# Other groupings of tokens in the loads, wider weight pieces and 128-row stores in a pooled attention with a feed-forward layer

## The chip, the cores and the metric

The kernel runs on one core of a Trainium2 chip. The metric is the device time of one execution in microseconds (us); the time before is the median of three runs.

## The reference

```python
def _attn_ref(q, k, v):                      # each [8, 8, 576, 64], float32
    B, H, S, D = q.shape
    pool = 8; Sp = S // pool                 # 72 pooled keys
    k_p = k.reshape(B, H, Sp, pool, D).mean(axis=3)
    v_p = v.reshape(B, H, Sp, pool, D).mean(axis=3)
    scores = np.matmul(q, k_p.transpose(0, 1, 3, 2)) / np.sqrt(D)
    attn = softmax(scores)                   # over the 72 pooled keys
    return np.matmul(attn, v_p)

def reference(q, k, v, moe_w_in, moe_w_out): # w_in [512, 2048], w_out [2048, 512]
    x = _attn_ref(q, k, v).transpose(0, 2, 1, 3).reshape(8 * 576, 512)
    h = x @ moe_w_in
    return (h * np.cos(h)) @ moe_w_out       # [4608, 512], float32
```

## The kernel before

The 4608 tokens are worked through in nine tiles of 512 (`TILE`), numbered t = 0 to 8. Tile t < 8 holds 512 of the 576 tokens of batch t; the remaining 64 tokens of each of the eight batches (`REST`) make up tile 8. A tile has an up stage (`up_mm`, L325: 64 matmuls of 512 columns with `w_in`, then cos on ScalarE at L332 and the product into `g_sb` on VectorE at L335) and a down stage (`down_mm`, L338: 64 matmuls with `w_out`, one block of 16 for each 128 tokens, called ms 0 to 3). `down_halves` (L344) splits a 128-row matmul of the down stage into two of 64 rows with results in different banks.

The attention of batch t + 1 is threaded into the down stage of tile t: the list `fill` says after how many down matmuls each piece is issued. For tiles 1 to 6 the order is `first_scores` after 4 matmuls, further `scores_of` at 11, 13 and 20, `values_rows` from 22 on. For tile 0 the list is longer, since batch 1's keys are pooled there too. Batch 0's attention is done ahead of everything, in the first 16 us. Each engine's queue runs in the order in which the program issues (`tc.manual_schedule`).

Loads: `load_q` brings a batch's q with 9 tokens (`ROW`) per partition and two heads side by side on the 128 partitions; `load_kv` brings keys or values with 8 tokens (one group to be pooled) per partition, 72 partitions, 8 heads after one another. They are issued on POOL's queue and cast to bfloat16 on the way. `w_in` comes in four pieces of 512 columns (`W_IN`), each in two requests. At most eight of POOL's requests are under way: the ninth waits for the first to land.

q is transposed by blocks of 128 columns, which hold two tokens of 64 elements each: `q_transpose_mm` (L214) on TensorE for batches 0 and 1, `q_transpose` (L206) by a transposing transfer on SP's queue for the others. After it, the lower 64 partitions of `qT` hold the even one of the two tokens and the upper 64 the odd one. `scores_mm` (L234) multiplies pooled keys `kk` (kept in both halves) with `qT`: for one head 256 columns from one half. With 9 tokens per partition a pair of heads begins at group 9 times the pair's number, an odd count of half-groups, so that half r alternates from pair to pair:

```python
pj, hp = divmod(h0 + i, 2)
g, r = divmod(ROW * pj + ORDER[c0 // 64], 2)
```

`scores_exp` (L244) takes exp on ScalarE, `values_rows` (L288 to L310) multiplies with the pooled values and sends the normalised rows to `xT` through a transposing transfer on SP's queue (L309). `k_transpose` (L185) makes `kk` from the pooled keys with another such transfer; for batch 1 `k_transpose_mm` (L192, copied at L194) does it on TensorE. POOL's `gate` (L493) waits for `kk` before it issues the next batch's loads. `down_out` (L347 to L358) copies a 128-token block out of PSUM into `o_sb` (six buffers) and stores it with two requests of 64 rows, each row of 2 KB; both are issued on SP's queue. In the last chunk (`last_chunk`, L366) the three pieces of a block go out on SP's and ScalarE's queues.

Of the kernel before, what the change touches and what calls it, by code (L numbers as in the profile page):

```python
# [19 lines left out]
def kernel(  # L20
# [22 lines left out]

    ORDER = (0, 2, 4, 6, 1, 3, 5, 7, 8)

# [14 lines left out]

    W_IN = ((0, 512), (512, 512), (1024, 512), (1536, 512))
    w_in_sb = [wpool.tile([128, KCH, n], BF16, name=f"w_in_sb{i}") for i, (c0, n) in enumerate(W_IN)]
# [26 lines left out]
    def kv_tile():  # L89
        return kvst.tile([128, 2 * H * POOL * D], BF16, name="kv_st", tag="kv_st")  # L90
# [9 lines left out]
    def q_tile(b):  # L100
        staged["q", b] = qst.tile([128, KCH, ROW, D], BF16, name="q_b", tag="q_b")

    def load_kv(b, which, src, h0=0, h1=H):

        if (which, b) not in staged:
            staged[which, b] = kv_tile()[:Sp].rearrange("p (i h t d) -> p i h t d", i=2, h=H, t=POOL)
        nc.gpsimd.dma_start(out=staged[which, b][:, 0, h0:h1].rearrange("p h t d -> p h (t d)"),
                            in_=src[b, h0:h1].rearrange("h (p t) d -> p h (t d)", t=POOL))

    def load_q(b):  # L110
        q_tile(b)
        load_even(staged["q", b], b, q)

# [13 lines left out]
    def w_in_cols(ki, fc):  # L127

        cg, r = divmod(fc, 4)
        return w_in_sb[cg][:, ki, :].rearrange("p (n r) -> p r n", r=4)[:, r]  # L130

# [56 lines left out]
    def k_transpose_mm(b, bank, h0, h1):  # L188

        ps = bank.bitcast(BF16)[:, 0:(h1 - h0) * Sp].rearrange("p (h n) -> p h n", n=Sp)  # L190
        for h in range(h0, h1):
            nc.tensor.matmul(ps[:, h - h0, :], kp2[b % 2][:Sp, h].rearrange("p s d -> p (s d)"), identity[:Sp, :Sp],  # L192
                             is_transpose=True)
        nc.vector.tensor_copy(out=kk[b % 2][:, h0:h1, 0:Sp], in_=ps)  # L194

    QB = KCH * ROW // 2

# [19 lines left out]
    def ex_col(u, i):  # L217

        (c0, n), (h0, nh) = u
        return (i // 2 % 2 * (nh // 2) + i // 4 * 2 + i % 2) * n  # L220

# [4 lines left out]
    def scores_mm(b, u, pair):  # L226
        (c0, n), (h0, nh) = u

        for i in [i + 2 * a for k in range(0, nh, 4) for i in (k, k + 1) for a in range(2)]:
            bank, c = divmod(ex_col(u, i), nh * n // 2)  # L230
            pj, hp = divmod(h0 + i, 2)
            g, r = divmod(ROW * pj + ORDER[c0 // 64], 2)
            ps = pair[bank][:Sp, c:c + n] if isinstance(pair, tuple) else pair[:Sp, bank, c:c + n]
            nc.tensor.matmul(ps.rearrange("p (g n) -> p g n", n=64),  # L234
                             lhsT=kk[b % 2][half[r], h0 + i, 0:Sp],
                             rhs=att["qT", b][half[r], g:g + n // 64, hp * 64:hp * 64 + 64])

    def scores_exp(b, u, pair):
# [3 lines left out]
        for src, c, m in ([(pair[:Sp, :, 0:w], 0, 2)] if not isinstance(pair, tuple) else  # L242
                          [(bank[:Sp, 0:w].unsqueeze(1), a * w, 1) for a, bank in enumerate(pair)]):
            nc.scalar.activation(out=ex[:, c:c + m * w].rearrange("p (a n) -> p a n", a=m), in_=src,  # L244
                                 func=ACTF.Exp, scale=scale / POOL)
        att["ex", b, u] = ex
# [40 lines left out]

    def values_rows(b, us_, blk, pair, m=128):  # L288

# [4 lines left out]
        for u in us_:  # L294
            (c0, n), (h0, nh) = u
            ex = att["ex", b, u]
            for i in range(nh):
# [10 lines left out]
        c = token(b, n0)  # L308
        nc.sync.dma_start_transpose(out=xT.rearrange("p e q n -> p (e q) n")[:, :, c:c + m],  # L309
                                    in_=x[:m].rearrange("p e h d -> p (e h d)"))  # L310

# [35 lines left out]
    def down_out(t, ms, ps, c0=0, queues=(nc.sync, nc.sync), other=None):  # L347
# [4 lines left out]
        else:  # L352
            nc.vector.tensor_copy(out=o[:, 0:n], in_=other)  # L353
            nc.vector.tensor_tensor(out=o[:, 0:n], in0=ps, in1=o[:, 0:n], op=ADD)
        rows_of = out.rearrange("(b p t) m -> b t p m", b=B, t=ROW)
        for i, rows in enumerate(half):
            b_, pos = (t, 2 * ms + i) if t < B else (2 * ms + i, ROW - 1)
            queues[i].dma_start(out=rows_of[b_, ORDER[pos], :, c0:c0 + n], in_=o[rows, 0:n])  # L358

# [28 lines left out]
    for rows in half:  # L388
# [4 lines left out]
                   allow_small_or_imprecise_dtypes=True)  # L393
    load_even(staged["q", 0], 0, q, 0, 2)
    load_even(staged["k", 0], 0, k, 2, 4)
    load_even(staged["q", 0], 0, q, 2, 4)
    load_even(staged["v", 0], 0, v, 0, 2)
# [18 lines left out]
    q_tile(1)  # L416
    for i in range(4):
        load_w_in(i)
    load_kv(1, "k", k, 0, 4)
    load_even(staged["q", 1], 1, q, 0, 2)  # L420
    load_w_out(0)
    load_kv(1, "k", k, 4, 8)
    load_w_out(1)
    load_even(staged["q", 1], 1, q, 2, 4)
    for i in range(2):
# [71 lines left out]
    for t in range(NT):  # L497
# [69 lines left out]
        if t == 0:  # L567
            fill = [(4, lambda: values_rows(0, [REST], 0, bk[0], 64)),
                    (12, lambda: k_transpose_mm(1, bk[1][:, 0, :], 0, 4)), (13, pool_k),
                    (16, scores_of((1, us[0], 0), (1, us[1], 1))), (22, late_q),  # L570
                    (26, lambda: k_transpose_mm(1, bk[1][:, 0, :], 4, 8)), (27, batch_2),
                    (29, scores_of((1, us[2], 0), (1, us[3], 1))), (29, pool_v), (49, sums_values),
                    (53, lambda: q_transpose(2)), (57, values_rest)]
        elif b < B:
# [90 lines left out]
```

## Time and profile before

| | |
|---|---|
| time, median of 3 runs (lowest to highest) | 292.0 us (291.92 to 293.37) |
| the profiled execution: time, span | 291.55 us, 289.4 us |
| TensorE clock granted | 0.999 |
| busy: PE, DVE, ACT, POOL | 281.9, 169.9, 142.2, 139.7 us |
| L325 (up), 576 matmuls | 126.1 us |
| L338 (down, whole array), 462 matmuls | 110.5 us |
| L234 (scores), 192 matmuls | about 15 us by their own ends |
| software queue (POOL's loads) | 18.07 MB, 40.1% of 16 engines |
| hardware queue (stores, transposes, first keys) | 18.10 MB, 34.5% |

Matmuls overlap, so the busy times of single ones add up to more than they take one after another; the chain of waits gives the time that each group took on the path. A queue's share is the time of its packets over 16 engines' span.

### The profile page before, as it was taken

The numbers are of one execution on the slowest core, as the hardware profiler recorded it, in microseconds if no ns is written. First come the engines' busy times: TensorE is split into PE (matmuls) and PEld (weight loads), VectorE is DVE, ScalarE is ACT, GpSimd is POOL, SyncE is SP. The second block draws the span as 40 slices with busy tenths as digits, with TensorE's granted clock in tenths as the row PEclk, the third lists the DMA queues.
The fourth block names the chain that finished last, engine by engine and source line by source line (L and its number), as shares of the span: only waits on it lengthen the run. The fifth ranks groups of instructions, "written<-read, shape, count | busy, mean of one in ns | idle before, by whom it ended". The sixth has DMA issues, their size and how long they took to land.

```text
span 289.4 us, 4907 instructions
## 1 busy us (share of the span) xinstructions
PE 281.9 (97%) x1989; PEld 147.1 (51%) x1989; DVE 169.9 (59%) x227; ACT 142.2 (49%) x142; POOL 139.7 (48%) x107
## 2 busy tenths in 40 slices
PE   7899999999999999999999999999999999999994
PEld 2655445555554555555555545554555454445444
DVE  5467849774757574658375737583666557216622
ACT  3786634678056904691369316841676066016400
POOL 8549525997973498369633993399000000000000
PEclk9999999999999999999999999999999999999999
DMA  7999999999976998696869976985603510230033
GB/s 151 196 202 208 207 194 166 202 136 179 193 148 86 179 142 181 90 162 128 166 70 167 160 150 103 175 146 116 131 1 74 119 36 2 50 82 14 0 72 74
DMA packets 58614, 36.60 MB, mean 126 GB/s; under 512 B 37984, under 2 KB 53344, under 8 KB 58592
## 3 DMA queue, kind: packets, MB, share of 16 engines
q0 software_dynamic: 18832, 18.07, 40.1%
q1 hardware_dynamic: 39520, 18.10, 34.5%
q8 instruction: 15, 0.25, 0.3%
q10 hardware_dynamic: 240, 0.13, 0.2%
q14 instruction: 7, 0.06, 0.1%
HBM read 36.70 MB, written 9.44 MB: 159 GB/s over the span
## 4 chain that ended last, share of the span: by engine, by line
PE 90%; DMA 6%; ACT 2%; DVE 0%; issue 0%; POOL 0%; POOLq 0%
PE bank L325 43%; PE obank L338 25%; PE bank L338 6%; PE obank L344 5%; DMA w_out_sb<-in_moe_w_out_dram 4%; PE bank L303 3%; PE bank L234 3%; DMA q_b<-in_q_dram 2%; PE bank L344 2%; ACT ex L244 1%; PE bank L366 1%; PE bank L272 1%; PE bank L263 0%; ACT cos L332 0%; DVE g_sb L335 0%
## 5 line engine op out<-in xcount | busy, mean ns | idle before, releaser
L332 ACT ACTIVATE cos<-bank,half_pi 128x1024 f32<-128x1024 f32 x72 | 80.4, 1118 | 115.4 <-PE bank L325 115.4
L325 PE MATMUL bank<-xT,w_in_sb 128*128 128x512 bf16 x576 | 126.1, 379 | 0.0
L335 DVE TENSOR_TENSOR g_sb<-bank,cos 128x1024 bf16<-128x1024 f32 x72 | 88.1, 1225 | 48.8 <-ACT cos L332 48.7
L325 PEld LDWEIGHTS <-w_in_sb 128*128 128x128 bf16 x576 | 65.1, 113 | 59.2 <-issue 0.6
L338 PE MATMUL obank<-w_out_sb,g_sb 128*128 128x512 bf16 x360 | 83.5, 379 | 0.0
L338 PEld LDWEIGHTS <-g_sb 128*128 128x128 bf16 x462 | 41.9, 97 | 45.9 <-issue 2.0
L146 POOL TENSOR_TENSOR kv_st<-kv_st 72x2048 f32<-72x2048 bf16 (+1 forms) x13 | 50.9, 3912 | 24.5 <-DMA kv_st<-in_k_dram 24.5
L244 ACT ACTIVATE ex<-bank 72x1024 bf16<-72x1024 f32 x32 | 30.4, 1019 | 4.7 <-PE bank L234 4.7
L351 DVE COPY o_sb<-obank 128x512 f32<-128x512 f32 x21 | 14.4, 690 | 30.3 <-PE obank L338 27.4
L149 POOL TENSOR_TENSOR kv_st<-kv_st 72x1024 f32<-72x1024 f32 (+1 forms) x13 | 29.5, 2268 | 1.0
L338 PE MATMUL bank<-w_out_sb,g_sb 128*128 128x512 bf16 x102 | 27.0, 379 | 0.1
L307 DVE TENSOR_TENSOR x_r<-bank,inv_r 128x512 bf16<-128x512 f32 (+1 forms) x32 | 22.1, 689 | 2.4 <-DMA xT<-x_r 1.4
L344 PE MATMUL obank<-w_out_sb,g_sb 64*128 64x512 bf16 x144 | 18.3, 376 | 0.0
L152 POOL TENSOR_TENSOR kp<-kv_st 72x512 bf16<-72x512 f32 (+1 forms) x14 | 16.4, 1189 | 0.6
L344 PEld LDWEIGHTS <-g_sb 64*128 64x128 bf16 x196 | 9.8, 94 | 7.3
L234 PE MATMUL bank<-qT,kk 64*72 64x256 bf16 (+1 forms) x184 | 13.1, 249 | 0.2
L234 PEld LDWEIGHTS <-kk 64*72 64x72 bf16 x192 | 8.5, 111 | 7.6 <-issue 3.3
L303 PEld LDWEIGHTS <-ex 72*128 72x128 bf16 x192 | 8.7, 97 | 6.2 <-ACT ex L244 1.7
L304 DVE RECIPROCAL inv_r<-bank 128x8 f32<-128x8 f32 (+1 forms) x32 | 6.5, 203 | 8.2 <-PE bank L303 7.5
L353 DVE COPY o_sb<-obank 128x512 f32<-128x512 f32 x6 | 4.2, 692 | 11.9 <-PE obank L344 11.9
L313 ACT ACT_TABLE_LOAD x8 | 10.3, 1283 | 0.9 <-PEq L649 0.7
L316 ACT ACT_TABLE_LOAD x8 | 10.3, 1283 | 0.1
(76 smaller groups left out, 148.5 us busy)
## 6 DMA issues: line engine op xcount, KB each, us to landing
out_dram<-o_sb SPq DMA_DIRECT2D x70, 128.0 KB, 2.4
kv_st<-in_k_dram POOLq DMA_DIRECT2D x6, 576.0 KB, 7.8
q_b<-in_q_dram POOLq DMA_DIRECT2D x6, 576.0 KB, 10.5
kv_st<-in_v_dram POOLq DMA_DIRECT2D x6, 576.0 KB, 13.4
w_in_sb<-in_moe_w_in_dram POOLq DMA_DIRECT2D x8, 256.0 KB, 10.5
w_out_sb<-in_moe_w_out_dram POOLq DMA_DIRECT2D x4, 512.0 KB, 11.2
q_b<-in_q_dram POOLq DMA_DIRECT2D x4, 288.0 KB, 9.0
kv_st<-in_v_dram POOLq DMA_DIRECT2D x4, 288.0 KB, 9.1
```

The costliest lines, as they stand in the source:

```text
L146: add(out=s, in0=x[:, :, 0:4, :], in1=x[:, :, 4:8, :], op=ADD)
L149: add(out=s[:, :, 0:2, :], in0=s[:, :, 0:2, :], in1=s[:, :, 2:4, :], op=ADD)
L152: add(out=kp2[b % 2][:Sp, h0:h1, slot, :], in0=s[:, :, 0, :], in1=s[:, :, 1, :], op=ADD)
L234: nc.tensor.matmul(ps.rearrange("p (g n) -> p g n", n=64), lhsT=kk[b % 2][half[r], h0 + i, 0:Sp], rhs=att["qT", b][half[r], g:g + n // 64, ...
L244: nc.scalar.activation(out=ex[:, c:c + m * w].rearrange("p (a n) -> p a n", a=m), in_=src, func=ACTF.Exp, scale=scale / POOL)
L303: nc.tensor.matmul(out[:, o0:o0 + D + 1], lhsT=ex[:, c:c + 128], rhs=v1)
L307: nc.vector.tensor_mul(out=x[:m].rearrange("p e h d -> p h e d"), in0=vals, in1=scale_of)
L325: nc.tensor.matmul(h[:, j, :], lhsT=w_in_cols(ki, fc), rhs=xT[:, ki % 2, ki // 2, t * TILE:(t + 1) * TILE], start=(ki == 0), stop=(ki == K ...
L332: nc.scalar.activation(out=cos, in_=h, func=ACTF.Sin, bias=half_pi[:, :1])
L335: nc.vector.tensor_mul(out=g_sb[:, 2 * fp:2 * fp + 2, :], in0=h, in1=cos)
L338: nc.tensor.matmul(o, lhsT=g_sb[:, fc, ms * 128:(ms + 1) * 128], rhs=w_out_sb[fc // 4][:, fc % 4, :], start=(fc == 0), stop=(fc == FFCH - 1))
L344: nc.tensor.matmul(ps, lhsT=g_sb[rows, fc, ms * 128:(ms + 1) * 128], rhs=w_out_sb[fc // 4][rows, fc % 4, :], start=start, stop=stop)
```

## The change

- q is loaded with 18 tokens per partition (`QROW`) and four heads side by side, in one request per batch (two for batches 0 and 1). A head's 512 tokens are then 256 even ones (lower half of `qT`) and 256 odd ones (upper half), and the 64 remaining ones are the last group, 32 in each half. `scores_mm` takes all heads of a unit from one half; the rest's scores become 16 matmuls of 32 columns in place of 8 of 64.
- The keys of batch 1 are loaded with two groups per partition. The order of the pooled keys is put right in the copy of `k_transpose_mm`.
- `w_in` comes in three pieces, the last one of 1024 columns.
- A store of 128 rows is one request; the tokens of a block lie as 4 tokens (two apart) times 32 partitions' worth of rows. In the last tile there are still two requests for a block, each of 2 x 32 rows.
- The transposing transfer of batch 0's rest is issued at place 54 of tile 0's list, not with its product at place 4.

```diff
-    ORDER = (0, 2, 4, 6, 1, 3, 5, 7, 8)
+    QROW = S // 32
-    W_IN = ((0, 512), (512, 512), (1024, 512), (1536, 512))
+    W_IN = ((0, 512), (512, 512), (1024, 1024))
...
     def load_kv(b, which, src, h0=0, h1=H):
+        if (which, b) == ("k", 1):
+            nc.gpsimd.dma_start(out=staged[which, b][:, 0, h0:h1].rearrange("p (j g) t d -> p j (g t d)", g=2),
+                                in_=src[b, h0:h1].rearrange("(j a) (p g t) d -> (a p) j (g t d)", a=2, g=2, t=POOL))
+            return
...
-    def load_q(b):
-        q_tile(b)
-        load_even(staged["q", b], b, q)
+    def load_q(b, j0=0, j1=2):
+        if ("q", b) not in staged:
+            q_tile(b)
+        nc.gpsimd.dma_start(out=staged["q", b][:, j0:j1].rearrange("p j t d -> p j (t d)"),
+                            in_=q[b, 4 * j0:4 * j1].rearrange("(j a) (p t) d -> (a p) j (t d)", a=4, t=QROW))
...
     # k_transpose_mm
-        nc.vector.tensor_copy(out=kk[b % 2][:, h0:h1, 0:Sp], in_=ps)
+        dst = kk[b % 2][:, h0:h1, 0:Sp].rearrange("q (j a) (p g) -> q j g a p", a=2, g=2)
+        src = ps.rearrange("q (j g) (a p) -> q j g a p", a=2, g=2)
+        nc.vector.tensor_copy(out=dst, in_=src)
...
     def scores_mm(b, u, pair):
-        for i in [i + 2 * a for k in range(0, nh, 4) for i in (k, k + 1) for a in range(2)]:
-            bank, c = divmod(ex_col(u, i), nh * n // 2)
-            pj, hp = divmod(h0 + i, 2)
-            g, r = divmod(ROW * pj + ORDER[c0 // 64], 2)
...
+        if u == REST:
+            parts = [(i, r, 8, r, i * 32, 32) for i in range(nh) for r in range(2)]
+        else:
+            order = [i + 2 * a for k in range(0, nh, 4) for i in (k, k + 1) for a in range(2)]
+            parts = [(i, c0 // 256, 0) + divmod(ex_col(u, i), nh * n // 2) + (n,) for i in order]
+        for i, r, g, bank, c, m in parts:
+            jq, a = divmod(h0 + i, 4)
+            g += 9 * jq
+            ps = pair[bank][:Sp, c:c + m] if isinstance(pair, tuple) else pair[:Sp, bank, c:c + m]
+            nc.tensor.matmul(ps.rearrange("p (g n) -> p g n", n=32),
                              lhsT=kk[b % 2][half[r], h0 + i, 0:Sp],
-                             rhs=att["qT", b][half[r], g:g + n // 64, hp * 64:hp * 64 + 64])
+                             rhs=att["qT", b][half[r], g:g + m // 32, a * 32:a * 32 + 32])
...
     def scores_exp(b, u, pair):
+            if u == REST:
+                dst = ex[:, 0:2 * w].rearrange("p (h a n) -> p a h n", a=2, n=32)[:, c // w:c // w + m]
+                src = src.rearrange("p a (h n) -> p a h n", n=32)
...
     # down_out
-        rows_of = out.rearrange("(b p t) m -> b t p m", b=B, t=ROW)
+        rows_of = out.rearrange("(b p t) m -> b t p m", b=B, t=QROW)
+        if t < B:
+            r, g = divmod(ms, 2)
+            nc.sync.dma_start(out=rows_of[t, 8 * g + r:8 * g + r + 7:2, :, c0:c0 + n], in_=o[:, 0:n])
+            return
         for i, rows in enumerate(half):
-            b_, pos = (t, 2 * ms + i) if t < B else (2 * ms + i, ROW - 1)
-            queues[i].dma_start(out=rows_of[b_, ORDER[pos], :, c0:c0 + n], in_=o[rows, 0:n])
+            queues[i].dma_start(out=rows_of[2 * ms + i, QROW - 2:QROW, :, c0:c0 + n], in_=o[rows, 0:n])
...
-            fill = [(4, lambda: values_rows(0, [REST], 0, bk[0], 64)),
+            fill = [(4, lambda: values_rows(0, [REST], 0, bk[0], 64, False)),
...
-                    (53, lambda: q_transpose(2)), (57, values_rest)]
+                    (53, lambda: q_transpose(2)), (54, lambda: att["put"]()), (57, values_rest)]
```

More of the change, by code (lines that the diff above doesn't have):

```diff
@@ L100, in q_tile @@
     def q_tile(b):
-        staged["q", b] = qst.tile([128, KCH, ROW, D], BF16, name="q_b", tag="q_b")
+        staged["q", b] = qst.tile([128, 2, QROW, D], BF16, name="q_b", tag="q_b")
     def load_kv(b, which, src, h0=0, h1=H):
@@ L129, in w_in_cols @@
         cg, r = divmod(fc, 4)
-        return w_in_sb[cg][:, ki, :].rearrange("p (n r) -> p r n", r=4)[:, r]
+        i = min(cg, 2)
+        c0 = (cg - i) * 512
+        return w_in_sb[i][:, ki, c0:c0 + 512].rearrange("p (n r) -> p r n", r=4)[:, r]
     att = {}
@@ L193, in k_transpose_mm @@
                              is_transpose=True)
-        nc.vector.tensor_copy(out=kk[b % 2][:, h0:h1, 0:Sp], in_=ps)
-    QB = KCH * ROW // 2
+        dst = kk[b % 2][:, h0:h1, 0:Sp].rearrange("q (j a) (p g) -> q j g a p", a=2, g=2)
+        src = ps.rearrange("q (j g) (a p) -> q j g a p", a=2, g=2)
+        nc.vector.tensor_copy(out=dst, in_=src)
+    QB = QROW
     def qT_tile(b):
@@ L219, in ex_col @@
         (c0, n), (h0, nh) = u
+        if u == REST:
+            return i * n
         return (i // 2 % 2 * (nh // 2) + i // 4 * 2 + i % 2) * n
@@ L227, in scores_mm @@
         (c0, n), (h0, nh) = u
-        for i in [i + 2 * a for k in range(0, nh, 4) for i in (k, k + 1) for a in range(2)]:
-            bank, c = divmod(ex_col(u, i), nh * n // 2)
-            pj, hp = divmod(h0 + i, 2)
-            g, r = divmod(ROW * pj + ORDER[c0 // 64], 2)
-            ps = pair[bank][:Sp, c:c + n] if isinstance(pair, tuple) else pair[:Sp, bank, c:c + n]
-            nc.tensor.matmul(ps.rearrange("p (g n) -> p g n", n=64),
+        if u == REST:
[8 more added lines that the diff above has]
+            nc.tensor.matmul(ps.rearrange("p (g n) -> p g n", n=32),
                              lhsT=kk[b % 2][half[r], h0 + i, 0:Sp],
-                             rhs=att["qT", b][half[r], g:g + n // 64, hp * 64:hp * 64 + 64])
+                             rhs=att["qT", b][half[r], g:g + m // 32, a * 32:a * 32 + 32])
     def scores_exp(b, u, pair):
@@ L243, in scores_exp @@
                           [(bank[:Sp, 0:w].unsqueeze(1), a * w, 1) for a, bank in enumerate(pair)]):
-            nc.scalar.activation(out=ex[:, c:c + m * w].rearrange("p (a n) -> p a n", a=m), in_=src,
-                                 func=ACTF.Exp, scale=scale / POOL)
+            if u == REST:
+                dst = ex[:, 0:2 * w].rearrange("p (h a n) -> p a h n", a=2, n=32)[:, c // w:c // w + m]
+                src = src.rearrange("p a (h n) -> p a h n", n=32)
+            else:
+                dst = ex[:, c:c + m * w].rearrange("p (a n) -> p a n", a=m)
+            nc.scalar.activation(out=dst, in_=src, func=ACTF.Exp, scale=scale / POOL)
         att["ex", b, u] = ex
@@ L286, in x_mul, with values_rows @@
         nc.vector.tensor_mul(out=xT[:, :, q, c:c + n], in0=ps[:, 0], in1=inv.unsqueeze(1).to_broadcast([128, 2, n]))
-    def values_rows(b, us_, blk, pair, m=128):
+    def values_rows(b, us_, blk, pair, m=128, now=True):
         n0 = us_[0][0][0] + blk * 128
@@ L308, in values_rows, with put @@
         c = token(b, n0)
-        nc.sync.dma_start_transpose(out=xT.rearrange("p e q n -> p (e q) n")[:, :, c:c + m],
-                                    in_=x[:m].rearrange("p e h d -> p (e h d)"))
+        def put():
+            nc.sync.dma_start_transpose(out=xT.rearrange("p e q n -> p (e q) n")[:, :, c:c + m],
+                                        in_=x[:m].rearrange("p e h d -> p (e h d)"))
+        if now:
+            put()
+        else:
+            att["put"] = put
     def exp_tables():
@@ L393 @@
                    allow_small_or_imprecise_dtypes=True)
-    load_even(staged["q", 0], 0, q, 0, 2)
+    load_q(0, 0, 1)
     load_even(staged["k", 0], 0, k, 2, 4)
-    load_even(staged["q", 0], 0, q, 2, 4)
+    load_q(0, 1, 2)
     load_even(staged["v", 0], 0, v, 0, 2)
@@ L416 @@
     q_tile(1)
-    for i in range(4):
+    for i in range(len(W_IN)):
         load_w_in(i)
     load_kv(1, "k", k, 0, 4)
-    load_even(staged["q", 1], 1, q, 0, 2)
+    load_q(1, 0, 1)
     load_w_out(0)
@@ L423 @@
     load_w_out(1)
-    load_even(staged["q", 1], 1, q, 2, 4)
+    load_q(1, 1, 2)
     for i in range(2):
```

## The prediction

> **What bounds the kernel now.** First the page's engines, then the chain of waits in order of time.
>
> ```profile
> PE 281.9 (97%) x1989; PEld 147.1 (51%) x1989; DVE 169.9 (59%) x227; ACT 142.2 (49%) x142; POOL 139.7 (48%) x107
> ```
>
> ```profile
> 15.97 12.37 PE bank L325 x56
> ...
> 43.33 0.04 issue
> ...
> 123.41 0.86 PE obank L338 x4
> 124.27 0.48 PE bank L234 x12
> 124.75 1.51 PE obank L344 x14
> 126.26 0.22 PE bank L234 x4
> ```
>
> TensorE works without a gap from 15.97 to 285.5 us; 43.33 is the only spot where a transfer (`w_out`'s last quarter) ends just when it is wanted. So all TensorE work added behind 15.97 is paid in full, work taken from other engines there is worth nothing, and a transfer matters only if it becomes late. Ahead of 15.97 the waits of TensorE show one transfer:
>
> ```profile
> PE bank L214 <- DMA q_b<-in_q_dram: 0.7, 1, 0.7
> ```
>
> Next, SP's queue in the timeline around one stage's end (up at 109.6, down at 123.4, next up at 139.74, next down at 153.55), and POOL's wait there:
>
> ```profile
> 129.26 1.11 SPq L358 DMA_DIRECT2D out_dram<-o_sb  x2
> 130.74 5.78 SPq L309 DMA_TRANSPOSE xT<-x_r  x4
> 136.62 1.18 SPq L358 DMA_DIRECT2D out_dram<-o_sb  x2
> 137.89 1.21 SPq L309 DMA_TRANSPOSE xT<-x_r  x1
> 139.20 2.46 SPq L358 DMA_DIRECT2D out_dram<-o_sb  x4
> 141.76 2.79 SPq L206 DMA_TRANSPOSE qT<-q_b  x1
> 144.64 1.27 SPq L185 DMA_TRANSPOSE kk<-kp  x1
> ```
>
> ```profile
> 148.87 0.18 POOL L493 COPY gate<-kk 1x1 bf16<-1x1 bf16 x1 [6.71 <-DMA kk<-kp]
> ```
>
> Stores and transposes share SP's queue: each `xT`, `qT` and `kk` stands behind stores. `kk` has landed at 148.87; the next stage's first scores want it at 154.41 (0.86 into the down stage). That slack of 5.5 us is what slower stores may eat. Last, two stretches (columns: length, PE, PEld, DVE, ACT, POOL, clock, DMA share, GB/s), the first with nothing but stores, the second with nothing but loads, and the issues' landing times:
>
> ```profile
> 246.00:258.00 12.00, 12.00 (x57) 5.50 (x56) 2.64 (x5) 0.00 (x0) 0.00 (x0) 1.00 0.30 66
> 16.00:28.00 12.00, 12.00 (x56) 6.22 (x57) 7.61 (x8) 9.39 (x12) 8.78 (x13) 1.00 1.21 206
> ```
>
> ```profile
> out_dram<-o_sb SPq DMA_DIRECT2D x70, 128.0 KB, 2.4
> ```
>
> Stores: 66 GB/s over 12 us is 792 KB or 387 rows of 2 KB; 0.30 of 16 engines' 12 us is 57.6 us, so a row holds an engine 149 ns. Loads: 206 GB/s is 2414 pieces of 1 KB written (2 KB read) in 192 us of engine time, 80 ns each.
>
> **Scores (L234), certain.** Today neighbouring heads read `qT` from opposite halves of the partitions (9 groups per pair of heads is odd), so two 64-row matmuls run side by side: four of 256 columns take 0.22 us. L344 shows the same (14 of 512 columns in 1.51 us, 0.108 each, against 0.216 for a whole-array one at L338). In the change the half is `c0 // 256`, one half for all four heads of a unit, so nothing pairs: 4 x 0.108 = 0.43, +0.21 a unit. Batches 1 to 7 have 28 units in the gapless stretch: 5.9 us. The rest of 64 tokens becomes 16 matmuls of 32 columns instead of 8 of 64; such short ones go at 21 ns (36 of L164 in 0.77) to 33 ns (8 in the 0.26 us that the rests take of the 0.48 above), so 0.17 to 0.26 each, seven times 1.2 to 1.8; I take 1.5. Sum 7.4 us.
>
> **Head.** The first q request has 128 rows of 4608 B, not 256 of 2304. POOL's 0.88 us to issue it falls towards `w_out`'s 0.55 to 0.58 (128 rows too): 0.3 us, and at most the 0.69 us that TensorE waits. Against it batch 0's units feed ACT's exp directly (8.68 to 9.09, 12.75 to 13.01), 0.21 later twice: +0.42. Net between -0.5 and +0.5, I take 0. The bytes are unchanged and the loads' stretch above has no gap (share over 1), so I count no faster transfer.
>
> **Wide w_in.** POOL waits for the third to sixth piece at 17.72, 18.99, 20.27 and 21.59, so the eighth lands near 24.2. Chunk pair 4 starts at 15.97 + 32 x 0.216 = 22.9 and wants the second half of K at 23.3, now part of the last wide piece: 0 to 0.9 us of stall, I take 0.5.
>
> **Free by cover.** Batch 1's wider keys (POOL waits for earlier landings, not for issue), the scattered copy at L194 (0.31 us of DVE; at worst doubled, where the scores at 34.34 follow 0.3 us later), exp's scattered output (ACT 49% busy). The deferred `xT` transpose of batch 0's rest leaves 33.83 and goes onto SP's queue behind batch 2's q transpose, ahead of four stores and `kk`'s transpose: 1.28 us, against 3.1 us between `kk` (60.36) and its use (63.44); its data is read only in the last tile.
>
> **Stores.** One request of 128 rows replaces two of 64, saving SP about 0.5 us each, off the path. But the row addresses no longer form one dimension: DRAM's side counts 4 x 32 rows, and 2 x 32 in the last tile. Every request of the trace leads with 64, 72 or 128 equal steps, which sixteen engines can share; if the leading count is what is split, 4 engines, and 2 at the end, take all. The trace shows no such request. Bounds: sixteen engines (no cost), or four with 32 rows each at 80 to 149 ns: 2.6 to 4.8 us a store instead of 1.2. I take four engines, as nothing in the leading count of 4 offers more, and 149 ns, the row of the same transfer. The Trainium skill, "DMA: Bandwidth & Descriptors", section "Why a DMA increments its semaphore by 16 and not by 1", speaks against the change: a transfer uses the largest count up to 16 that divides the slowest dimension of both sides, from the lowest engines on, so 4 and 2; no row here shows it, and the sum by it is the one below. The same skill, "SBUF — State Buffer", section "Door 1: The DMA port swizzle", says that 64 adjacent partitions reach half of the ports, which would explain 149 against 80 ns; by it a 128-row store over sixteen engines would cost half as much a row.
>
> On those four engines a stage holds: stores 4 x 4.8 = 19.2; transposes 8 (SP's queue has 34.5% of the span; 4608 stored rows x 149 ns are 14.8%; the other 19.7% is 57 us an engine over seven batches); loads 1.77 MB at 206 GB/s, 8.6. That is 36 us, where the stage lasts 30.14 (154.41 from 124.27) + 1.05: +4.8 at least. Followed in order, with loads and stores alternating: a store after ms 0 and the `xT` transposes end 2.5 us past the next up, three stores follow back to back (14.4), then q and `kk` (141.76 to 148.87, less issue, 5.7): a period of about 39.5, +8.3. I take the sum, since some rows should go faster than 149: 5 stages (t = 2 to 6) x 4.8 = 24. In stage 1, `kk` stands behind two stores, 9.6 us, less the 1.2 they take now and slack, about 4 late. The last tile: its first store is issued at 275.8; six requests of 32 rows an engine take 28.6, six of the last chunk (two at a half, four at a quarter row) 9.5, so the data ends at 275.8 + 1.8 (2.4 less four rows) + 38.1 = 315.7; now the last is issued at 285.9 and landed 2.1 later. +28.
>
> **Sum.** The profiled execution took 291.55 us with a span of 289.4, 0.45 under the median: 292.0 + 7.4 + 0.5 + 24 + 4 + 28 = 356 us.
>
> **Rivals.**
> 1. Four engines, but rows at 80 ns, since four engines crowd less: the stage's sum is 10.2 + 8 + 8.6 = 27, under 31.2, no stall; the tail is 275.8 + 1.8 + 20.5 = 298.1, +10. 292 + 7.9 + 10 = 310, to 325 where the order costs 3 us a stage. For it: the loads' row; against: the same kind of row takes 149.
> 2. The request is spread over sixteen (the change does not do what I fear): 292 + 7.9 = 300, 298 to 302. For it: total bytes and rows are the same.
> 3. Not slower: the scores still pair, because a unit's matmuls run beside those of the other half in L344's sequence or in the next unit. Then 7.4 goes to nothing, and with sixteen engines and 0.5 us from q it is 291.5. It decides if over nine tenths of the 28 units hide. Against: the chain's pieces come one after another in program order, and the neighbours are eight matmuls at most.
>
> **How the numbers follow.** Four engines near 149 ns 0.53, rival 1 0.21, rival 2 0.23, rival 3 0.02, other 0.01. A difference of 0.5% (1.5 us) is about what a measurement can tell here. The range goes from rival 2's lower end less 1, 297, to the chain's 8.3 instead of 4.8 (356 + 17.5), with a little for loads, 376. Faster 0.01, same 0.01, slower 0.98.
>
> **What would show it.** Scores: four L234 in 0.43, not 0.22. Stores: landing of the 256 KB request 5 to 7 us against 2.4; SP's queue share up in the few engines; waits of L234 and L325 for `kk<-kp`, `qT<-q_b` or `xT<-x_r` in stages 1 to 6, and an end behind the last matmul of tens of us that waits for `out_dram`. If stores land in about 2 us, rival 2 holds; if chains of four L234 stay at 0.22, I am wrong on the part that I call certain.

## The result and the profile after

| | before | after |
|---|---|---|
| median | 291.96 us (291.84 to 293.37, 4 executions) | 328.49 us (324.68 to 333.16, 4 executions) |
| profiled execution: time, span | 291.55, 289.4 us | 324.68, 322.7 us |
| TensorE clock granted, mean | 0.999 | 0.972 |

The change makes the kernel slower by a factor of 1.113 (95% interval 1.106 to 1.119). The factor compares 324.68 and 325.82 us with the kernel before; two executions with a still lower clock (331.15 and 333.16) are left out of it, though longer waits inside the stages can bring the clock down by themselves, as the second profile of this kernel below (329.82 us, clock 0.956) shows. The forecast was 356 us with a range of 297 to 376. Everything below is in spans of profiled executions: 322.7 - 289.4 = 33.3 us more.

The page of the changed kernel: the engines, the two hardware queues (packets, MB, share of 16 engines) and the group of stores.

```profile
PE 285.4 (88%) x2019; PEld 157.1 (49%) x2053; DVE 169.5 (53%) x227; ACT 143.1 (44%) x142; POOL 137.6 (43%) x105
...
q1 hardware_dynamic: 38498, 18.09, 37.4%
...
q10 hardware_dynamic: 198, 0.13, 0.1%
...
out_dram<-o_sb SPq DMA_DIRECT2D x32, 256.0 KB
```

TensorE's busy time grew by 3.5 us only, but its share fell from 97% to 88%: most of the 33 us is idle time that was not there before. The waits of TensorE name it (us in total, times, longest):

```profile
PE bank L353 <- DMA xT<-x_r: 5.8, 3, 2.4
PE bank L353 <- DVE x_r L329: 4.1, 1, 4.1
PE bank L252 <- DMA kk<-kp: 2.4, 2, 1.9
```

That is 12.3 us in which an up stage (L353, L325 before) or the first scores (L252, L234 before) stood for a transposing transfer: L329 is the writing of `x_r`, and VectorE's own waits have 20.6 us in all there, for `xT` transfers that still read the buffer. Before, TensorE waited for no transfer after the head. SP's queue in the timeline, around tile 1's down stage (65 to 83 us), shows what the transposes stand behind:

```profile
56.27 2.61 SPq L195 DMA_TRANSPOSE kk<-kp  x1
58.92 13.51 SPq L386 DMA_DIRECT2D out_dram<-o_sb  x3
74.11 8.78 SPq L333 DMA_TRANSPOSE xT<-x_r  x4
82.98 1.17 SPq L386 DMA_DIRECT2D out_dram<-o_sb  x2
```

(A line joins neighbouring issues of one kind; its length runs from the first one's start to the last one's end, waits for the data included.) The four `xT` transposes take SP 8.78 us, against 5.78 in the lines shown of before. The chain of waits for the same place (start, length, what) ends in the up stage of tile 2:

```profile
56.27 9.88 DMA kk<-kp
...
74.11 11.23 DMA xT<-x_r
...
87.00 4.43 PE bank L353 x10
```

Windows of TensorE's clock around that wait (columns as in the prediction; the clock is the third number from the end) show a second cost:

```profile
83.00:87.00 4.00, 0.00 (x1) 0.11 (x1) 1.53 (x4) 0.00 (x0) 3.92 (x4) 0.88 1.14 140
87.00:92.00 5.00, 4.78 (x11) 1.73 (x12) 0.74 (x2) 1.11 (x1) 4.92 (x2) 0.50 0.76 114
92.00:96.00 4.00, 4.00 (x18) 1.96 (x17) 2.25 (x2) 1.86 (x2) 1.36 (x2) 0.89 0.73 146
```

After 4.1 us without a matmul the clock is at half for 5 us and short of full for some more: 0.50 x 5 + 0.11 x 4 = 2.9 us lost, on top of the wait. The Trainium skill, "TensorE: Matmul & The Clock Gate", section "What's actually happening", has half clock after an idle window of about 3.4 us, and this trace agrees: the waits of 1.2 to 2.5 us further on leave the clock at 1.00. But the length of a wait alone does not decide. In e10_stage32 below, a wait of 2.15 us in tile 1, shorter than the page's window, is followed by a clock of 0.50 (82.8 to 85.0 us) and 0.71 (85.0 to 87.0), and the measurement decides; in e6_lead8, one of 2.17 us at the same place left it at 1.00. What makes the difference was not tried.

Last, the end. The chain of waits ends with the last chunk and its copy; behind it there is nothing but stores, whose DMA share in the window from the last matmul on stands last but one:

```profile
302.53 3.55 PE bank L397 x48
...
306.10 0.29 DVE o_sb L379
```

```profile
306.10:322.70 16.60, 0.00 (x0) 0.00 (x0) 0.29 (x1) 0.00 (x0) 0.00 (x0) 0.66 0.11 41
```

0.11 of 16 engines is 1.8, as if the last tile's stores went through two engines; the next section shows that they do. The span ends 16.6 us after the last matmul; before it was 289.4 - 285.5 = 3.9.

Put together from the starts of the up stages in the two chains: the head +1.0; the stages +19.6 (12.3 of waits, 2.9 of clock, 6 x 0.67 = 4.0 of scores, worked out below, less 0.2 in tile 0, and 0.6 not assigned); the end +12.7. Sum 33.3.

### The profile page after: what moved, and what is told of

Its sections match the earlier page's. It is cut to its first block, busy times and chain, and to the rows that moved or that the text cites. A ratio compares the mean times of both kernels' runs of the same rounds, so it can differ in the third digit from the quotient of the medians.

```text
span 322.7 us, 4967 instructions
## 1 busy us (share of the span) xinstructions
PE 285.4 (88%) x2019; PEld 157.1 (49%) x2053; DVE 169.5 (53%) x227; ACT 143.1 (44%) x142; POOL 137.6 (43%) x105
## 3 DMA queue, kind: packets, MB, share of 16 engines
q1 hardware_dynamic: 38498, 18.09, 37.4%
## 4 chain that ended last, share of the span: by engine, by line
PE 70%; DMA 15%; DVE 4%; ACT 3%; issue 1%; SPq 1%; POOL 0%; POOLq 0%; DVEq 0%
PE bank L353 34%; PE obank L366 15%; DMA xT<-x_r 8%; PE bank L366 7%; PE obank L372 5%; DMA kk<-kp 4%; PE bank L252 4%; DMA q_b<-in_q_dram 2%; PE bank L325 2%; PE bank L372 2%; DVE g_sb L363 2%; ACT cos L360 1%; ACT ex L267 1%; PE bank L397 1%; DVE x_r L329 1%
## 5 line engine op out<-in xcount | busy, mean ns | idle before, releaser
L353 PE MATMUL bank<-xT,w_in_sb 128*128 128x512 bf16 x565 | 128.3, 385 | 10.6 <-DMA xT<-x_r 5.8
L353 PEld LDWEIGHTS <-w_in_sb 128*128 128x128 bf16 x576 | 65.3, 114 | 72.4 <-issue 12.9
L366 PE MATMUL obank<-w_out_sb,g_sb 128*128 128x512 bf16 x345 | 81.9, 379 | 0.7 <-issue 0.2
L267 ACT ACTIVATE ex<-bank 72x1024 bf16<-72x1024 f32 x32 | 31.2, 1017 | 8.6 <-PE bank L252 8.5
L329 DVE TENSOR_TENSOR x_r<-bank,inv_r 128x512 bf16<-128x512 f32 (+1 forms) x32 | 22.1, 689 | 21.5 <-DMA xT<-x_r 20.6
L366 PE MATMUL bank<-w_out_sb,g_sb 128*128 128x512 bf16 x95 | 25.6, 379 | 1.0 <-issue 1.0
L379 DVE COPY o_sb<-obank 128x512 f32<-128x512 f32 x21 | 14.0, 683 | 20.6 <-PE obank L366 20.5
L252 PE MATMUL bank<-qT,kk 64*72 64x256 bf16 (+1 forms) x240 | 18.8, 231 | 3.5 <-DMA kk<-kp 2.4
L372 PE MATMUL obank<-w_out_sb,g_sb 64*128 64x512 bf16 x144 | 21.4, 377 | 0.0
L252 PEld LDWEIGHTS <-kk 64*72 64x72 bf16 x256 | 14.2, 112 | 9.4 <-DMA kk<-kp 3.6
L372 PEld LDWEIGHTS <-g_sb 64*128 64x128 bf16 x196 | 17.0, 94 | 2.6
L524 POOL COPY gate<-kk 1x1 bf16<-1x1 bf16 x5 | 0.9, 181 | 39.3 <-DMA kk<-kp 39.3
L162 POOL TENSOR_TENSOR kp<-kv_st 72x512 bf16<-72x512 f32 (+1 forms) x14 | 16.3, 1187 | 0.5
L325 PEld LDWEIGHTS <-ex 72*128 72x128 bf16 x192 | 9.2, 97 | 5.7
```

The lines of the kernel that those rows point to most:

```text
L162: add(out=kp2[b % 2][:Sp, h0:h1, slot, :], in0=s[:, :, 0, :], in1=s[:, :, 1, :], op=ADD)
L252: nc.tensor.matmul(ps.rearrange("p (g n) -> p g n", n=32), lhsT=kk[b % 2][half[r], h0 + i, 0:Sp], rhs=att["qT", b][half[r], g:g + m // 32, ...
L267: nc.scalar.activation(out=dst, in_=src, func=ACTF.Exp, scale=scale / POOL)
L325: nc.tensor.matmul(out[:, o0:o0 + D + 1], lhsT=ex[:, c:c + 128], rhs=v1)
L329: nc.vector.tensor_mul(out=x[:m].rearrange("p e h d -> p h e d"), in0=vals, in1=scale_of)
L353: nc.tensor.matmul(h[:, j, :], lhsT=w_in_cols(ki, fc), rhs=xT[:, ki % 2, ki // 2, t * TILE:(t + 1) * TILE], start=(ki == 0), stop=(ki == K ...
```

## How many engines a store uses

Two readings need no further kernel. The first counts packets. Bytes are the same to 0.01 MB, but queue 1 has 39520 - 38498 = 1022 packets fewer and ScalarE's queue 10 has 240 - 198 = 42 fewer. Suppose that each engine that takes part in a request adds one packet for its completion. Before, SP issued 73 stores: 73 x 16 = 1168. After, it issued 32 of 128 rows and 9 in the last tile: 32 x 4 + 9 x 2 = 146. The difference is 1022. ScalarE's three requests: 3 x 16 - 3 x 2 = 42. Both fit to the packet; with 8 and 4 engines, say, the first difference would be 1168 - 32 x 8 - 9 x 4 = 876. This is the count that the Trainium skill's rule ("DMA: Bandwidth & Descriptors", the section cited in the prediction) gives for leading counts of 4 and 2.

The second is the flow while stores alone are under way, in the DMA view: 40 slices of the window, GB/s. First before (246 to 258 us), then the kernel e5_flat128 below, which stores 128 rows over sixteen engines (254 to 262 us), then e3_tail32, whose stages store as the change does (276 to 290 us), then e2_before_lead2, with a leading count of 2 (310 to 322 us), and last the changed kernel in its last tile, whose requests read 64 partitions with a leading count of 2 (300 to 310 us).

```profile
GB/s 0 0 0 0 0 0 0 0 0 0 0 218 198 225 198 34 0 0 0 0 0 0 109 205 198 225 137 0 0 0 0 0 0 0 218 198 219 198 41 0
```

```profile
GB/s 358 399 379 103 0 82 0 0 0 0 0 0 0 0 0 0 0 338 379 369 226 0 0 0 0 0 0 0 0 0 0 0 0 0 225 369 410 297 10 0
```

```profile
GB/s 53 18 6 53 64 76 105 99 94 111 88 47 18 64 59 76 105 105 99 99 88 41 12 76 64 94 99 111 94 117 59 23 18 59 64 99 99 111 94 88
```

```profile
GB/s 48 55 55 48 48 55 55 48 48 55 55 48 48 55 55 14 0 0 0 0 0 0 0 0 0 0 0 14 27 14 48 34 27 27 27 20 48 41 55 48
```

```profile
GB/s 49 33 33 49 57 49 49 57 49 49 49 49 49 57 49 57 49 49 49 49 41 25 49 41 0 0 25 25 49 49 49 49 57 57 49 49 45 49 53 49
```

The full flow is about 210, 380, 100, 51 and 49 GB/s. With 16, 16, 4, 2 and 2 engines that is 156, 86, 82, 80 and 84 ns for a row of 2 KB. So a row that is stored from all 128 partitions takes about 84 ns, however many engines write at once. A row from 64 partitions takes 149 to 156 ns with sixteen engines at work, but 84 with two: it is neither the 64 partitions nor the sixteen engines alone, but both together. The DRAM rows do not do it either, as e2_before_lead2 writes the rows of the kernel before at 80 ns. This fits the half-the-ports rule which the prediction quoted and did not use: sixteen engines stay at about 210 GB/s on half of the partitions, and two engines, at 49, are far below that.

## The experiments

The theory is the forecast's: 4 and 2 engines make the stores slow, and what waits behind them on SP's queue reaches TensorE. The rivals are a layout of the DRAM rows that is slow by itself, and costs that belong to q, the scores or `w_in`.

**All stores in requests of 32 rows** (e1_rows32), so that no leading count is below 32; the last tile's two requests are split in the same way.

```diff
-            nc.sync.dma_start(out=rows_of[t, 8 * g + r:8 * g + r + 7:2, :, c0:c0 + n], in_=o[:, 0:n])
+            for s in range(4):
+                nc.sync.dma_start(out=rows_of[t, 8 * g + r + 2 * s, :, c0:c0 + n], in_=o[32 * s:32 * s + 32, 0:n])
```

> The changed kernel, but every store in requests of 32 rows (one token position, 32 rows of equal step): leading count 32, so sixteen engines can share each. Theory (the stores' leading count confines them to 4 and 2 engines): the waits for xT and kk in the stages go (about 17 us), the end behind the last matmul falls from 16.6 us to about 4; what is left of the change is the head (+1.0) and the scores (+0.66 a stage): 292 + 1 + 4 = 297 us, 296 to 299. Rival (the new q layout, its larger pieces or the order of the queue delay the transposes): over 318 us, with only the end shorter. Rival (more requests cost SP): 16 issues a stage of 0.5 us, waits for kk of some us a stage, 300 to 310.

Measured: 300.1 us (298.0 to 302.2), 1.026 times before (1.015 to 1.036); span 296.3. The median is 1 us above the 296 to 299 expected, at the lower edge of the rival that more requests cost SP; of that rival's waits for `kk` there is none. TensorE's waits for `kk` are gone and one of 1.2 us for `x_r` is left. The output lies in the same places as with the change, so 26 of the 33 us come from the form of the requests and not from where the rows lie.

**The last tile alone in requests of 32 rows** (e3_tail32) **and the stages alone** (e10_stage32), each half of the edit above.

> The changed kernel, with requests of 32 rows in the last tile alone; the stores of 128 rows in tiles 0 to 7 stay. Theory: only the end shrinks, from 16.6 us behind the last matmul to about 4, so 325 - 12.7 = 312 us (310 to 315), and the waits of tiles 1 to 6 stay as they are. Rival (the end waits for a backlog of the 128-row stores of tile 7): the end stays above 10 us and the time above 320.

> The changed kernel with the stores of tiles 0 to 7 in four requests of 32 rows each and the last tile's stores left as the change has them (six requests whose leading count is 2 plus the last chunk). Theory that stalls of the stages and the end add up: the kernel with all stores in 32-row requests took a span of 296.3 us; the last tile's two engines put the end 16.6 us behind the last matmul where that one had about 4, so 296.3 + 12.6 less the 1.5 of its own queue at the end = 307 to 309 of span, 309 to 312 us, no wait of TensorE for kk and at most one for xT. Rival, that the last tile's layout also moves the stages (the kernel with only the last tile in 32-row requests won 6 us, not the 12.6 that its end became shorter): about 324.7 less 6 less 17 of stalls is not reached, and this one ends near 318, with waits for xT or kk of several us in tiles 2 to 6.

Measured: e3_tail32 318.8 us (1.087, 1.076 to 1.098), e10_stage32 312.2 us (1.066, 1.060 to 1.072). Both ends did what was expected: 316.6 - 311.8 = 4.8 us behind the last matmul with 32-row requests, 310.7 - 294.0 = 16.7 without. e10_stage32 has three up stages in its chain that begin exactly 30.81 us apart, with no wait for a transfer between them:

```profile
115.41 13.81 PE bank L353 x64
...
146.22 13.81 PE bank L353 x64
...
177.03 13.81 PE bank L353 x64
```

Its span is e1_rows32's plus 14.4 (10.7 to 12.7 were expected): 11.9 at the end, 1.0 because it waits 2.2 us for `x_r` in tile 1 instead of 1.2, and 1.6 of clock behind that wait (an up stage of 15.62 us instead of 13.97). So the end's cost adds to the rest, and the rival to that, 318 us, is out. e3_tail32 missed: 312 was expected. Its end won 11.8 us, but its stages, the same code as in the changed kernel, took 5.7 us more: its last matmul ends at 311.8 where the changed kernel's ends at 306.1. The waits of TensorE in it are

```profile
PE bank L252 <- DMA kk<-kp: 6.4, 3, 5.0
PE bank L353 <- DMA xT<-x_r: 4.3, 1, 4.3
PE bank L353 <- DVE o_sb L379: 4.2, 1, 4.2
```

14.9 us instead of 12.3, and three single ones of 4.2 to 5.0 us, each of which brought the clock down (0.50 in the 4 us behind the first, 0.60 in the 4 behind the second, 0.52 in the 5 behind the third).

**The changed kernel a second time** (e11_after_again), since that left open whether the stages' waits are fixed.

> The changed kernel, unchanged, a second time. Theory that the stalls of the stages vary from execution to execution, because stores, transposes and loads meet on the same few engines in an order that small delays shift: between tiles 2 and 6 the stages' lengths differ by several us from the first profile's (39.3, 32.0, 32.2, 33.1, 33.8, 30.8 from tile 1 on), their sum lies within 12 to 30 us over 30.8 a stage, and the end stays at 16.6 behind the last matmul to within 0.5. Rival, that the order of the program fixes them: the same lengths to within 0.5 each.

Measured: 326.1 to 333.8 us, profiled at 329.82 with a span of 327.9 and a clock of 0.956. The end is 16.6 us again. The waits have moved: from the up stage of tile 1 on, the stages are 38.2, 36.4, 32.9, 34.6, 32.9 and 31.0 us long, where the first profile has 37.4, 33.9, 32.0, 33.1, 33.8 and 31.0; over 30.81 a stage that is 21.1 us against 16.3. (The expectation has 39.3 and 32.0 for the first two: the same 71.3 us, divided 1.9 us later.) The rival, fixed stages, falls. But it isn't free play either. The chains of this run and of e3_tail32 in order, first this run's, then e3_tail32's:

```profile
124.50 15.90 PE bank L353 x64
...
192.04 15.66 PE bank L353 x64
```

```profile
124.50 5.54 PE bank L353 x17
...
192.25 6.14 PE bank L353 x17
```

The up stages of tiles 3 and 5, and that of tile 6 (224.97 and 225.53), begin at nearly the same times in both, with waits of 3.8 to 5.0 us ahead of the first two in both (15.90 and 15.66 us where an up stage behind a short wait takes 13.98 are the slow clock behind them). So the same stores fall into at least two patterns of waits, 5 us apart, and e3_tail32's profile has the second one: 327.9 - 11.8 = 316.1, and it took 316.6. Its expectation had been worked out from the first. What decides between the patterns is open.

**Stores over sixteen engines** (e5_flat128): the change with its 128 rows at one equal step, so written to other places of the output.

```diff
-        rows_of = out.rearrange("(b p t) m -> b t p m", b=B, t=QROW)
+        rows_of = out.rearrange("(p t) m -> t p m", t=36)
-            nc.sync.dma_start(out=rows_of[t, 8 * g + r:8 * g + r + 7:2, :, c0:c0 + n], in_=o[:, 0:n])
+            nc.sync.dma_start(out=rows_of[4 * t + ms, :, c0:c0 + n], in_=o[:, 0:n])
-            queues[i].dma_start(out=rows_of[2 * ms + i, QROW - 2:QROW, :, c0:c0 + n], in_=o[rows, 0:n])
+            queues[i].dma_start(out=rows_of[4 * t + ms, 64 * i:64 * i + 64, c0:c0 + n], in_=o[rows, 0:n])
```

> The changed kernel, with stores of 128 (last tile 64) rows to rows of equal step, so that the leading count is 128: the output's rows are written to other places than the reference has them, bytes and requests are those of the change. Theory: sixteen engines share a request, 297 us (296 to 299), below or equal to the kernel with 32-row requests. A row then holds an engine about 84 ns if the 149 ns of the kernel before come from rows of one half of the partitions, and about 149 ns if they come from sixteen engines writing at once. Rival (one request of 256 KB is itself slow, however it is spread): over 318 us.

Measured: 295.99 us, 1.008 (1.005 to 1.012), span 293.9, so a request of 256 KB is not slow by itself. No wait for `xT` or `kk` is left; everything else of the change is in it. So all else in the change costs 4.5 us of span: 4.0 for the scores, 0.6 for a later head (first up stage at 16.59 instead of 15.97), 0.3 for the wide `w_in`, less 0.5 at the end (293.9 - 290.5 = 3.4 behind the last matmul); these make 4.4. The comparison has less, 0.8% or 2.3 us: the kernel before took 293.8 in the median on that chip, 1.9 more than in the first runs, and why was not looked into. One of its waits, 0.3 us for `w_in_sb` in tile 0's up stage, belongs to the wide `w_in`. Queue 1's share, with the same data, is 27.6%, below the 34.5% of before, as rows of 86 ns instead of 149 should make it. And q's transposing transfer, in the same new layout, holds SP for 2.8 us in the median of six, as before, where the changed kernel's six have 8.1: the slow stores lengthen it, not the layout.

**Eight engines** (e6_lead8): e5_flat128 with the stages' stores as 8 x 16 rows.

```diff
-            nc.sync.dma_start(out=rows_of[4 * t + ms, :, c0:c0 + n], in_=o[:, 0:n])
+            by_8 = out.rearrange("(b p t) m -> b t p m", b=B, t=36)
+            nc.sync.dma_start(out=by_8[t, 8 * ms:8 * ms + 8, :, c0:c0 + n], in_=o[:, 0:n])
```

> As the kernel with stores of equal step (leading count 128), but the 128-row stores of tiles 0 to 7 go to 8 x 16 rows (again to other places than the reference has them); the last tile's stay at equal step. Theory: eight engines with 16 rows each, 1.3 us a store; they hold 5.4 + 8 + 8.6 = 22 us of work in a stage of 30.8, so no wait: 296 us (295 to 298), and the hardware queue has 256 fewer completion packets (32 stores x 8) than with leading count 128. Rival (any store with two row dimensions is slow): 305 us or more.

Measured: 297.5 us (1.013, 1.006 to 1.021), span 296.3. Queue 1 has 38752 packets, 256 = 32 x 8 fewer than e5_flat128's 39008: eight engines each. So the rival, that any store with two row dimensions is slow (305 us or more), is out. Its stages are back at 30.81 us; one wait of 2.2 us for `x_r` in tile 1, where none was expected, is all that is left. Its span is 2.4 us above that with sixteen engines. That this is the price of eight engines is not shown: e10_stage32 has the same wait with sixteen engines in its stages. The four and two engines of the change cost 322.7 - 293.9 = 28.8.

**The kernel before with the suspected form** (e2_before_lead2): its two requests of 64 rows become one whose leading count is 2, nothing else is changed.

```diff
+        if t < B:
+            a = ORDER[2 * ms]
+            nc.sync.dma_start(out=rows_of[t, a:a + 3:2, :, c0:c0 + n], in_=o[:, 0:n])
+            return
         for i, rows in enumerate(half):
```

> The kernel before with one part of the change: a store of 128 rows is one request (two token positions times 64 rows), leading count 2, in tiles 0 to 7; the last tile as before. Theory: two engines with 64 rows each at 84 ns, 5.4 us a store; these engines hold 21.5 + 8 + 8.6 = 38 us of work a stage of 30.1, so stages 1 to 6 take 6 to 12 us longer each and the time is 330 to 365 us, tail unchanged. Rival (spread over sixteen whatever the leading count): 290 to 293.

Measured: 360.3 us, 1.228 (1.215 to 1.241). The same 128 rows, in fewer requests, cost 358.0 - 289.4 = 68.6 us of span. Queue 1 has 38560 packets, 960 fewer than before: 64 requests x 16 engines less 32 x 2. TensorE's waits in it:

```profile
PE bank L325 <- DMA xT<-x_r: 20.5, 3, 8.3
PE bank L234 <- DMA kk<-kp: 14.9, 6, 5.8
PE bank L325 <- DVE o_sb L351: 10.8, 1, 10.8
PE bank L325 <- DVE x_r L307: 7.1, 1, 7.1
```

The third says that the up stage at 225.73 us waits for a copy out of PSUM (L351). VectorE's timeline shows why that copy is late:

```profile
224.38 0.68 DVE L307 TENSOR_TENSOR x_r<-bank,inv_r 64x512 bf16<-64x512 f32 x1 [13.41 <-DMA xT<-x_r]
224.99 1.27 DVE L351 COPY o_sb<-obank 128x512 f32<-128x512 f32 x2
```

VectorE itself stood 13.41 us for a buffer that an `xT` transfer still read, and the copy is queued behind. So this wait for `o_sb`, like those for `x_r`, is a wait for `xT` seen at another place. The clock is 0.924 on average. This is the run that shows the cause without q, scores or weights.

**The scores moved together** (e9_pair): e5_flat128, with the second unit of scores issued right before the third, so that units of opposite halves are neighbours.

```diff
-            fill = [(4, first_scores), (11, scores_of((b, us[1], 1))),
-                    (13 + 2 * d, scores_of((b, us[2], 2))), (20 + d, scores_of((b, us[3], 1))),
+            fill = [(4, first_scores),
+                    (13 + 2 * d, scores_of((b, us[1], 1), (b, us[2], 2))), (20 + d, scores_of((b, us[3], 1))),
```

> As the kernel with stores of equal step, but the second unit of scores (lower half) is issued right before the third (upper half) in tiles 1 to 6. Theory that two units of opposite halves, issued after one another, run side by side (as the eight of batch 1 did in 0.57 us): the second costs nothing, 0.21 us a stage less, 1.3 us in all, 294.7. Rival (matmuls start strictly one after another, the pair of units in batch 1 being an exception of the idle array): no change, 296.

Measured: 295.67 us, 1.007 (1.004 to 1.010), where 294.7 was expected; a stage lasts 30.72 us instead of 30.81. The two times differ by less than their intervals, so the chain has to decide. Here is why it won so little: the chain of e5_flat128 in one down stage, L252 being scores and L372 the split down matmuls (L344 before).

```profile
126.47 0.69 PE bank L252 x18
127.15 0.11 PE obank L372
127.26 0.11 PE bank L252
127.37 1.51 PE obank L372 x13
128.88 0.22 PE bank L252 x2
129.10 0.11 PE obank L372
129.21 0.11 PE bank L252
...
129.53 0.02 PE bank L252
...
130.53 0.86 PE bank L372 x8
131.39 0.44 PE bank L252 x4
```

the same stretch of before, which the prediction shows up to 126.26:

```profile
126.91 0.22 PE bank L234 x4
...
127.78 0.86 PE bank L344 x8
128.64 0.22 PE bank L234 x4
```

and that of e9_pair around its pair of units:

```profile
96.84 1.94 PE obank L372 x17
98.78 0.47 PE bank L252 x8
99.25 0.65 PE obank L372 x6
```

What a unit costs is read from the start of one unit to that of the next. The first unit, with the rest's 16 short matmuls and the L372 behind it, takes 128.88 - 126.47 = 2.41 us (1.99 before); the second, with its L372, 0.65 (0.65 before); the third 1.00 (0.87); the last, which stands alone, 0.44 (0.22). So the first and the last pay in full, +0.42 and +0.22, and the two middle ones +0.13 together: an L372 matmul of the other half goes in between their fours, and the row halves of neighbouring instructions run side by side across the border of the two groups. Eight of opposite halves, none alternating, take 0.47, hardly more than two units of before (0.44). So moving the middle ones together could win only about 0.1 a stage, and 0.09 came.

**The wide `w_in` and the deferred transpose alone** (e8_before_win_put), on the kernel before.

```diff
-    W_IN = ((0, 512), (512, 512), (1024, 512), (1536, 512))
+    W_IN = ((0, 512), (512, 512), (1024, 1024))
...
-            fill = [(4, lambda: values_rows(0, [REST], 0, bk[0], 64)),
+            fill = [(4, lambda: values_rows(0, [REST], 0, bk[0], 64, False)),
...
-                    (53, lambda: q_transpose(2)), (57, values_rest)]
+                    (53, lambda: q_transpose(2)), (54, lambda: att["put"]()), (57, values_rest)]
```

> The kernel before with two parts of the change: w_in's second half in pieces of 1024 columns, and the transpose of batch 0's rest deferred. Theory: both are hidden; at most the last wide piece lands 0.5 us late for chunk pair 4: ratio 0.998 to 1.003. Rival (the deferral frees the loads before w_out's last quarter, or the wide piece stalls by 0.9 us and more): a change of over 0.5% either way.

Measured: 292.94 us, 0.999 (0.996 to 1.002). Both are hidden.

**The first q request in two of 9 tokens** (e7_q_half_rows), on e5_flat128, to see whether the longer rows delay the head.

```diff
-        nc.gpsimd.dma_start(out=staged["q", b][:, j0:j1].rearrange("p j t d -> p j (t d)"),
-                            in_=q[b, 4 * j0:4 * j1].rearrange("(j a) (p t) d -> (a p) j (t d)", a=4, t=QROW))
+        for t0, t1 in ((0, 9), (9, 18)) if (b, j0) == (0, 0) else ((0, QROW),):
+            nc.gpsimd.dma_start(out=staged["q", b][:, j0:j1, t0:t1].rearrange("p j t d -> p j (t d)"),
+                                in_=q[b, 4 * j0:4 * j1].rearrange("(j a) (p t) d -> (a p) j t d", a=4, t=QROW)[:, :, t0:t1].rearrange("p j t d -> p j (t d)"))
```

> As the kernel with stores of equal step, but the first q request is made as two, of 9 tokens (2304 B) per row each. If the larger rows make the first q land later (7.3 us before, 7.5 to 7.9 in the changed kernel's runs), it lands by 7.3 and the up stage begins 0.2 to 0.6 us earlier. If the landing only varies from run to run, or the second issue costs what the rows bring, it stays between 7.3 and 7.9. The time is 295 to 297 either way.

Measured: 295.27 us in a single execution, span 293.4; q's wait is gone from TensorE's waits and the first up stage starts at 15.99 us instead of e5_flat128's 16.59. It does not settle when q lands. e8_before_win_put, with q as before, waits 1.3 us for q and starts that stage at 16.45, so the landing varies by about as much as the layout could cost. What follows the landing is settled: from the first transpose of q to the first up matmul it is 8.62 us in the kernel before (7.33 to 15.95) and in e8_before_win_put, and 9.02 in the changed kernel (7.95 to 16.97) and in e5_flat128. These 0.4 us come with the change.

## Why the prediction was right, and why its number was 31 us too high

The direction, the engines and the kind of wait came as forecast. That the time lies in the range is in part luck: the range reaches down to the second rival, and the sum of 356 us, 31 above the profiled 324.68, rests on a price of a row that did not hold.

- **Engines: right.** 4 in the stages and 2 in the last tile, by the packets and by the flow. (Whether sixteen engines share the loads that lead with 72 equal steps, as the prediction has it, no run shows; nothing rests on it.)
- **The row of 149 ns: wrong, and the largest error.** The step "149 ns, the row of the same transfer" took the price of sixteen engines on 64 partitions for four engines on 128 and for two on 64. Measured: 80 to 86 ns. With 84 the sum for a stage is 4 x 32 x 84 ns = 10.8 of stores, 8 of transposes and 8.6 of loads, 27 us, under the 30.81 that a stage lasts; so the term of 5 x 4.8 = 24 falls. So the four engines were not the bound of the stages. What the stages pay are waits for transposes that stand behind one to three such stores, 2.7 us each: 12.3 us in six tiles. In stages 2 to 6, where the 24 were expected, the first profile has 9.7 us more than five times 30.81, clock included, and the second 13.7. That the stores' form causes these waits is shown (e1_rows32, e10_stage32, e2_before_lead2); whether a transpose loses its time on the shared engines or at its issue on SP was not tried apart.
- **Stage 1: near in number, in part by luck.** +4 expected for `kk`, beside the scores; +6.0 measured (37.41 from up to up, 30.72 before, less 0.67 of scores), but only 1.9 of it for `kk`, the other 4.1 through `xT` and `x_r`; and 2.9 of clock behind it, in tile 2.
- **The clock: not foreseen.** The forecast priced waits alone. Behind the waits of 3.8 to 5.0 us ahead of an up stage, that stage lost another 1.7 to 2.9 us to the clock.
- **Scores: certain, and too dear.** Expected 7 x 1.05 = 7.4. Measured 6 x (30.81 - 30.14) = 4.0: in a stage +0.42 for the first unit with the rest's 16 short matmuls, as counted, +0.13 for the two middle units together, +0.22 for the last, as counted, and 0.1 less elsewhere. In tile 0 nothing, as eight of opposite halves stand together there (0.57 us in the chain). The step "nothing pairs" failed for the middle units and in tile 0: pairing goes by the neighbours in the queue, not by the unit. The third rival named this mechanism; nearly half of the cost hid, where it needed over nine tenths.
- **Head: 0 expected, +1.0 measured**, of which 0.4 is the 0.42 that the prediction had counted for batch 0's units ahead of exp, and 0.6 a longer wait for q (1.3 against 0.7). The 0.3 that it set against them did not come: POOL issues the first q request in 0.74 us instead of 0.88, not in 0.55 to 0.58, and q lands no earlier. Why it lands later is not settled, see above. **Wide `w_in`:** 0.5 expected, 0.3 in e5_flat128, nothing on the path where the head is later.
- **The end: right in kind, +28 expected, +12.7 measured.** The same step: six requests of 32 rows an engine, from 64 partitions but through two engines, are 16.1 us at 84 ns, where 28.6 were counted.
- **Free by cover: held.** Neither batch 1's keys nor the L194 copy (L206 after) shows up among TensorE's waits, and e8_before_win_put has the deferred transpose at nothing.
- **The rivals.** The first (four engines, 80 ns, "310, to 325 where the order costs 3 us a stage") is what happened, at its upper end and, by the median of 328.49, above it. It had 0.21 against the forecast's 0.53. Its reason, that fewer engines crowd less, holds for the last tile: 84 ns with two engines on 64 partitions. A hint was in the text: 149 ns for rows of 64 partitions and 80 ns for pieces that went to all of them. I read the difference as one of stores against loads, though the second rule quoted explained it by the partitions. For two engines on 64 partitions no row of before gives the price.

No version beats the kernel before: e8_before_win_put equals it, e5_flat128 is 0.8% behind, most of it for the scores.

## What to carry to other kernels

When an edit merges requests, write down the shape of both sides before anything else: a leading count of 2 or 4 can leave 14 or 12 of 16 engines idle, and fewer, larger requests then cost more than many small ones (152 requests of 32 partitions came out 26 us better than the change's 44 here). A slow store is seldom the wait itself: look for what is queued behind it, here the transposes on the same queue, and look at the clock behind a longer wait of TensorE (it took another 1.7 to 2.9 us behind waits of 3.8 to 5.0 us here, and 1.6 once behind one of 2.2). Take the price of a row from a request with the same partitions and the same number of engines, not only of the same tensor.

## What the runs showed of the hardware

- A store of 2 KB rows took 80 to 86 ns a row and engine from 128 partitions with 2, 4 or 16 engines at work. From 64 partitions it took 149 to 156 with sixteen engines, and 84 with two. A 128-row request at an equal step therefore flows at about 380 GB/s, against 210 for its halves.
- Each engine that takes part in a request left one packet for its completion; the packet counts of the queues then give the engines to the unit (differences of 1022, 42, 960 and 256 in these runs).
- Matmuls on opposite row halves overlapped without alternating: four on one half, then four on the other, in 0.47 us, nearly as little as two alternating units of four took (2 x 0.22).
- 4.1 us of idle put the clock at 0.50 for 5 us; 2.5 us of idle did not move it in the same trace, but 2.15 us did in e10_stage32 (0.50 for 2.2 us, then 0.71 for 2).
- On a queue with slow stores the transposing transfer of q held SP for 9.46 us at its issue, against 2.79 before and 2.8 in e5_flat128 with the same layout of q. The line of the changed kernel's timeline:

```profile
122.68 9.46 SPq L218 DMA_TRANSPOSE qT<-q_b  x1
```

Why the issue itself takes longer was not tried.
